# Statistics, query weights and a key projection placed elsewhere in the opening of a pre-norm attention and bilinear GLU kernel

## The chip, the cores and the metric

The kernel runs on one core of one Trainium2 chip. The metric is the device time of one execution in microseconds (us); the numbers compared are medians of several executions. A core has TensorE (PE: matmuls, PEld: its weight loads), VectorE (DVE), ScalarE (ACT), GpSimd (POOL) and SyncE, which here issues all transfers (SPq). Each engine runs its own instructions in the order in which the program hands them out, and waits on semaphores for the others.

## The reference, cut to what matters

```
h  = x + A(layernorm(x)) ;  out = h + B(layernorm(h))        x: 2048 tokens x 576
A(x): q = x @ wq (32 heads of 18), k = x @ wk, v = x @ wv (one key and value head for all)
      softmax(q k^T * 18**-0.5) v, heads joined, @ wo
B(x): ((x @ w_gate) * (x @ w_up)) @ w_down                   width 4608
layernorm(x) = (x - mean) / sqrt(var + 1e-5)
```

Everything is fp32. Most products are done as two or three matmuls in the fast fp32r form, of a high part and a low remainder of each operand.

## The kernel before

The tokens are four blocks of 512, and each block four tiles of 128 (tile 7 is block 1's last, tile 11 block 2's last). `blocks` and `ffn` hold the long part: for each head group and each 128 keys a pair of scores on PE (`pair`: two steps `pr` = 0, 1), an exponential on ACT, and four matmuls with the values (`flush`), among which the GLU's matmuls are spread. Before that comes `keys_values`, the opening, some 60 us, in which every instruction's place is written by hand; all that the change touches lies there. There is no scheduler: the order of the calls is the order on every engine.

What the opening does for each block b of tokens:

- Mean and variance of each tile: `stats` (DVE, bn_stats twice and bn_aggr) or `stats_act` (ACT: a pass that sums, a small one that makes the bias, a pass of squares; the two passes write into a junk tile). `scale` makes 1/sqrt(var + eps) of several tiles in some 17 small instructions on POOL (or DVE). `apply` normalises two tiles on DVE (L204) and two on ACT (L206).
- `turns`: PE transposes the four tiles into PSUM, tiles tr (two, each two banks, tag "s") and trt (tag "m"). `parts`: ACT casts them into high parts (L88, L97), DVE makes the low parts (L89, L98); the result is XT of this block.
- `project(b)`: 14 matmuls psk give keys, values and the last four heads' queries. `keys(b)` makes from it kk (ACT L260), a copy kvq (ACT L262) and, by transfers, the kT that scores read. `values(lo, hi)`: PE transposes values into psv, and DVE copies them into V (L287).
- For block 0 also `query(i)`: 14 matmuls psq, i = 0 to 3, with the weights of seven heads each. These weights are cast by `highs` (the high part) and `lows` (the low part, POOL). `ready(i)` takes psq out of PSUM (cast, then DVE L89) and stores the queries; `bounds` (matmul psg) makes a bound of the scores for the softmax.

[...] Scores and tr share two double banks (tag "s"); trt, psb, psv of blocks after the first and psk of block 3 use one bank (tag "m"); the accumulator of the values has one (tag "a"), which psk of blocks 0 and 1 uses before; psq, the first psg and psk of block 2 share two banks (tag "f"). A tile of a tag takes a bank only when the last reader of the tile that had it is done:

```
    def ps_f(self, name):
        return self.ps.tile([P, TB], F32, tag="f", bufs=2, name=name)
```

`some(gen, n)` issues the next n steps of a generator, `drain` all that are left. `step(work, n)` is a first score, n steps of work, a second score, and the value matmuls of all pending 128 keys but the last. In the profile the scores are s (L608), the exponentials P (L609), the value matmuls acc (L613).

Of the kernel before, what the change touches and what calls it, by code (L numbers as in the profile page):

```python
# [54 lines left out]
class Block:  # L55
# [78 lines left out]
    def keys_values(self, others):  # L134

        pe, act, dve, sp, pool = self.pe, self.act, self.dve, self.sp, self.nc.gpsimd
# [35 lines left out]
        def stats(lo, hi):  # L172
            for j in range(lo, hi):
                b, s = divmod(j, NQ)
                self.ln_stats(xs[b][:, s, :], mv[:, j, :], s, f"a{b}")

        def stats_act(lo, hi):

            junk = self.pp.tile([P, D], F32, tag="P", name="lnjunk")
            x = lambda j: xs[j // NQ][:, j % NQ, :]  # L180
            for j in range(lo, hi):
                act.activation(junk, x(j), AF.Copy, scale=1.0 / D, accum_out=mv[:, j, 0:1])
            for j, less in zip(range(lo, hi), (kab, kabq)):
                act.activation(less, mv[:, j, 0:1], AF.Copy, scale=-1.0 / ROOT_D)
            for j, less in zip(range(lo, hi), (kab, kabq)):
                act.activation(junk, x(j), AF.Square, bias=less, scale=1.0 / ROOT_D, accum_out=mv[:, j, 1:2])

        def scale(lo, hi, eng):
            r = self.rstd(mv[:, lo:hi, 1], f"a{lo}", eng, hi - lo)
            n = self.lp.tile([P, NQ], F32, tag="n", name=f"n{lo}")[:, :hi - lo]  # L190
            if eng is pool:
                pool.tensor_tensor(n, mv[:, lo:hi, 0], r, ALU.mult)
                pool.tensor_scalar(n, n, -1.0, None, ALU.mult)
            else:
                dve.scalar_tensor_tensor(n, mv[:, lo:hi, 0], -1.0, r, ALU.mult, ALU.mult)
            for j in range(lo, hi):
                rs[j] = r[:, j - lo:j - lo + 1], n[:, j - lo:j - lo + 1]

        def apply(b, *of, on=None):
            for s in of:  # L200
                xh = xhs[s] = self.pp.tile([P, D], F32, tag="P", name=f"xh{b}_{s}") if b < 2 else xs[b][:, s, :]
                r, n = rs[NQ * b + s]
                if on is dve:
                    dve.tensor_scalar(xh, xs[b][:, s, :], mv[:, NQ * b + s, 0:1], r, ALU.subtract, ALU.mult)  # L204
                else:
                    act.activation(xh, xs[b][:, s, :], AF.Identity, bias=n, scale=r)  # L206
# [37 lines left out]
        def project(b):  # L244
            psk = psks[b] = (self.ps_a if b < 2 else self.ps_m if b == NB - 1 else self.ps_f)(f"psk{b}")
            for i, (w, m) in enumerate(highs_first(w_h, w_l, self.XT[b])):
                pe.matmul(psk[:6 * DH], w, m, start=(i == 0), stop=(i == 13))  # L247
                yield
# [33 lines left out]
        def values(lo, hi):  # L282
            psv = (self.ps_m if lo else self.ps_a)(f"psv{lo}").rearrange("p (t c) -> p t c", c=64)[:, 0:hi - lo]
            for t in range(lo, hi):
                b, q = divmod(t, NQ)
                pe.transpose(psv[:, t - lo, 0:44], self.kvq[KV, b, q * P:(q + 1) * P], self.ident[KV, KV])
            dve.tensor_copy(self.V[:, lo:hi, 1:1 + DH], psv[:, :, 44 - DH:44])  # L287

        def highs(i, cast):
            cast(self.wq_h[cols[i]], wqr[i])  # L290

        def lows(i):
            pool.tensor_tensor(self.wq_l[cols[i]], wqr[i], f32(self.wq_h[cols[i]]), ALU.subtract)

        def query(i):
            psq = psqs[i] = self.ps_f(f"psq0_{i}")
            for k, (w, m) in enumerate(highs_first(self.wq_h[cols[i]], self.wq_l[cols[i]], self.XT[0])):
                pe.matmul(psq[:7 * DH], w, m, start=(k == 0), stop=(k == 13))
                yield

        def ready(i, copy):
            qs = self.qb.tile([P, 2, TB], F32R, tag="qs", bufs=QS, name=f"qs0_{i}")
            self.split(qs[:7 * DH, 0], qs[:7 * DH, 1], psqs.pop(i)[:7 * DH], copy)
            if i == 0:
                yield
            yield from self.store_q(0, 7 * i, 7, qs, 0 if i else 4)

        def some(gen, n=1):
            for _ in range(n):
                next(gen, None)  # L310

        def step(work=iter(()), n=0):
            self.pair()
            some(work, n)
            self.pair()
            self.flush(len(self.pend) - 1)

        q0, q1, q2, q3 = (query(i) for i in range(4))
# [17 lines left out]
        lows(1)  # L336
        highs(2, act.copy)
        lows(2)
        stats(5, 8)
        scale(4, 8, pool)  # L340
        drain(project(0))
        mean()
# [7 lines left out]
        stats(9, 10)  # L350
        t0 = ready(0, act.copy)
        some(t0, 2)
        some(g0)
        some(t0)
        some(k0)
        some(q1, 6)
        self.bounds(0, act.copy, self.pp.tile([H, 2, TB], F32R, tag="P", name="m2_0"), G0)
        apply(1, 0, 1, on=dve)
        apply(1, 2, 3)
# [6 lines left out]
        some(t0)  # L366
        t1 = ready(1, act.copy)
        some(t1)
        stats(11, 12)
        scale(8, 12, pool)  # L370
        highs(3, pool.tensor_copy)
        lows(3)
        some(q2, 3)
        values(0, 4)
        turns(1)
        parts()
# [15 lines left out]
        some(t2)  # L392
        some(k1)
        some(q3, 4)
        step(q3, 0)
        values(4, 8)
        drain(project(2))
        apply(3, 0, 1, on=dve)
        apply(3, 2, 3)
        drain(t1)  # L400
# [5 lines left out]
        k2 = keys(2)  # L406
        some(k2, 3)
        self.last_heads(0)
        step()
        step(others, 2)  # L410
        drain(project(3))
        k3 = keys(3)
# [851 lines left out]
def f32(ap):  # L1264
    return ap.bitcast(F32)
# [10 lines left out]
def highs_first(W, Wl, XT):  # L1276

    p = passes(W, Wl, XT)
    return p[0:12:3] + p[2:12:3] + p[1:12:3] + p[12:]
# [7 lines left out]
def drain(gen):  # L1287
    for _ in gen:
        pass
# [76 lines left out]
```

## Time and profile before

| | |
|---|---|
| median of 3 runs | 2278.04 us (2277.4 to 2278.1) |
| the profiled execution | 2278.2 us, its span 2276.3 us (1.9 us lie outside the span) |
| PE busy | 2255.7 us, 99% |
| ACT, DVE, POOL busy | 1416.2, 1206.0, 758.9 us |
| granted TensorE clock, mean | 0.999 |

The span runs from the first to the last instruction. Busy times of PE have modelled ends, so "99%" says that PE has few long gaps, not that it streams at its peak. The times in the rows further on count from the start of the span.

### The profile page before, as it was taken

Reading aid. Unit: us, or ns where it says so; the run is one execution under the profiler, and the core shown is the slowest. Engines: PE = TensorE matmul, PEld = TensorE weight load, DVE = VectorE, ACT = ScalarE, POOL = GpSimd, SP = SyncE. Lnnn points to the kernel's source line nnn. Section 1 sums busy time; section 2 is a strip of 40 time slices with the busy share of each in tenths; the row PEclk is TensorE's granted clock in tenths of the full one; section 3 lists DMA queues with packets and bytes.
Section 4 is the critical chain, followed back from the end, with each engine's and each line's share of the span. In section 5 each row is a group of like instructions: output and inputs, shape, how many; then the busy total and the mean of one; then the engine's idle time right before and its main releaser. Section 6 shows DMA issues by size and latency. Waiting matters only on the chain.

```text
span 2276.3 us, 45913 instructions
## 1 busy us (share of the span) xinstructions
PE 2255.7 (99%) x18106; PEld 1602.0 (70%) x18106; DVE 1206.0 (53%) x2131; ACT 1416.2 (62%) x1844; POOL 758.9 (33%) x902
## 2 busy tenths in 40 slices
PE   8999999999999999999999999999999999999998
PEld 5433345777777767677777777777777788888887
DVE  7332435566656577444544455444445476566565
ACT  6899887666676666767666666666676533232332
POOL 4000003565565554232222232223222233333342
PEclk9999999999999999999999999999999999999999
DMA  5222314444333344533333343634333355655553
GB/s 176 84 75 72 112 30 137 152 137 151 136 125 127 137 159 141 205 116 123 115 119 104 121 135 119 194 126 125 104 121 109 122 171 178 209 172 172 181 187 109
DMA packets 127273, 306.75 MB, mean 135 GB/s; under 512 B 17569, under 2 KB 17697, under 8 KB 126409
## 3 DMA queue, kind: packets, MB, share of 16 engines
q1 hardware_dynamic: 127049, 303.73, 40.9%
q8 instruction: 145, 2.38, 0.4%
q14 instruction: 79, 0.65, 0.1%
HBM read 233.76 MB, written 55.67 MB: 127 GB/s over the span
## 4 chain that ended last, share of the span: by engine, by line
PE 95%; DVE 2%; DMA 1%; ACT 1%; issue 0%; SPq 0%; POOL 0%; DVEq 0%; ACTq 0%
PE acc L613 20%; PE pg L1002 20%; PE y L962 17%; PE gu L1002 13%; PE s L608 12%; PE pu L1002 6%; PE yo L766 3%; PE psq L460 2%; DMA X<-X 1%; PE y L920 1%; ACT P L609 1%; DMA x<-in_x_dram 0%; DVE XT L89 0%; PE psk L247 0%; PE ye L920 0%
## 5 line engine op out<-in xcount | busy, mean ns | idle before, releaser
L609 ACT ACTIVATE P<-s 128x1024 f32<-128x1024 f32 x1024 | 1035.7, 1027 | 282.4 <-PE s L608 185.4
L1002 PE MATMUL pg<-X,ws 64*128 64x512 f32 x2592 | 702.6, 389 | 0.1
L1002 PE MATMUL pu<-X,ws 64*128 64x512 f32 x2592 | 702.3, 389 | 0.2 <-DMA X<-X 0.2
L1002 PEld LDWEIGHTS pg<-X,ws 64*128 64x128 f32 x2592 | 479.3, 185 | 69.4 <-issue 1.2
L1002 PEld LDWEIGHTS pu<-X,ws 64*128 64x128 f32 x2592 | 477.2, 185 | 21.2 <-DVE h L767 1.3
L613 PE MATMUL acc<-P,V 128*32 128x512 f32 x4096 | 487.5, 598 | 0.0
L608 PE MATMUL s<-q,kT 56*128 56x512 f32 x2048 | 446.9, 416 | 2.3 <-ACT P L609 1.6
L962 PEld LDWEIGHTS y<-wdo,room 128*128 128x128 f32 x2856 | 386.1, 188 | 46.6 <-issue 45.8
L962 PE MATMUL y<-wdo,room 128*128 128x288 f32 x2856 | 402.7, 300 | 0.0
L969 ACT COPY tmp<-y 128x288 f32<-128x288 f32 x408 | 163.0, 400 | 329.7 <-PE y L962 313.2
L608 PEld LDWEIGHTS s<-q,kT 56*128 56x128 f32 x2048 | 209.4, 184 | 177.9 <-ACT P L609 95.1
L1002 PE MATMUL gu<-X,ws 64*128 64x512 f32 x2592 | 301.7, 389 | 0.6 <-DMA X<-X 0.6
L613 PEld LDWEIGHTS acc<-P,V 128*32 128x32 f32 x4096 | 114.0, 109 | 241.3 <-issue 231.3
L1002 PEld LDWEIGHTS gu<-X,ws 64*128 64x128 f32 x2592 | 246.7, 184 | 49.7 <-issue 4.7
L88 POOL CAST ws<-wr 128x1152 fp32r<-128x1152 f32 x144 | 172.5, 1198 | 319.9 <-PE pu L1002 165.0
L970 POOL TENSOR_TENSOR x<-x,tmp 128x288 f32<-128x288 f32 x204 | 159.2, 809 | 358.9 <-ACT tmp L969 358.1
L970 POOL TENSOR_TENSOR h<-h,tmp 128x288 f32<-128x288 f32 x204 | 159.1, 809 | 305.9 <-ACT tmp L969 305.5
L89 DVE TENSOR_TENSOR ws<-wr,ws 128x1152 fp32r<-128x1152 f32 x144 | 219.6, 1525 | 76.1 <-POOL ws L88 76.1
L1036 DVE TENSOR_TENSOR hf<-pu,g 128x512 f32<-128x512 f32 x96 | 66.3, 691 | 360.1 <-ACT g L1032 359.8
L965 DVE TENSOR_TENSOR x<-x,y 128x288 f32<-128x288 f32 x272 | 117.5, 453 | 146.4 <-PE y L962 146.4
L965 DVE TENSOR_TENSOR h<-h,y 128x288 f32<-128x288 f32 x272 | 118.2, 454 | 111.7 <-PE y L962 108.7
L88 ACT CAST room<-hf 128x256 fp32r<-128x256 f32 (+1 forms) x144 | 73.9, 513 | 55.9 <-DVE hf L1036 55.4
(182 smaller groups left out, 1676.8 us busy)
## 6 DMA issues: line engine op xcount, KB each, us to landing
wdo<-wd_dram SPq DMA_DIRECT2D x369, 288.0 KB
wr<-in_wgu_dram SPq DMA_DIRECT2D x144, 576.0 KB
wd_dram<-wdo SPq DMA_DIRECT2D x123, 288.0 KB
q<-q_dram SPq DMA_DIRECT2D x64, 216.0 KB
raw<-in_wd_dram SPq DMA_DIRECT2D x36, 288.0 KB
q_dram<-qs SPq DMA_DIRECT2D x15, 504.0 KB
X<-X SPq DMA_DIRECT2D x24, 256.0 KB
ob<-ob SPq DMA_DIRECT2D x121, 36.0 KB
```

What stands on the lines that cost most here:

```text
L88: (copy or self.cast)(hi, src)
L89: self.dve.tensor_tensor(lo, src, f32(hi), ALU.subtract)
L608: self.pe.matmul(s_[:, i], self.kT[o:o + 56, t * P:(t + 1) * P], q[o:o + 56, pr], start=True, stop=True)
L609: self.act.activation(p_, s_, AF.Exp, scale=SCALE)
L613: self.pe.matmul(acc[32 * j:32 * j + 32, :], self.V[:, t, :], Ps[j // 2][:, j % 2, :], start=(t == 0), stop=(t == NT - 1), skip_group_chec ...
L766: pe.matmul(y[:, :HD], m, k, start=(i == 0), stop=(i == len(ms) - 1))
L962: pe.matmul(y[:, :HD], m[:, t * P:(t + 1) * P], k, start=(first and j == 0), stop=(j == 2), skip_group_check=True)
L965: dve.tensor_tensor(hs, hs, y[:, :HD], ALU.add)
L969: act.copy(z, y[:, :HD])
L970: pool.tensor_tensor(hs, hs, z, ALU.add)
L1002: pe.matmul(ps, w[o:o + 64, wk, c], X[o:o + 64, xk, c], start=(j == 0), stop=(j == 26))
L1036: dve.tensor_tensor(hf, pu, g, ALU.mult)
```

## The change

Six edits, all in the opening:

1. The last query weights (i = 3) are cast by ACT (`highs(3, act.copy)`) right after those of i = 2, and their low part follows on POOL. Before, POOL did both later, behind `scale(8, 12)`.
2. The statistics of tile 7 go from DVE to ACT.
3. Those of tile 11 go from DVE to ACT, to a place behind the cast of the first query.
4. Eight in place of six matmuls of psq 1 stand ahead of the first `bounds`, and five in place of three of psq 2 ahead of `values(0, 4)`.
5. The key projection of block 2 stands between the two scores of a pair, in place of behind `values(4, 8)`.
6. At a later pair all pending value matmuls come between the two scores, in place of behind them.

```diff
         lows(2)
-        stats(5, 8)
+        highs(3, act.copy)
+        lows(3)
+        stats(5, 7)
+        stats_act(7, 8)
         scale(4, 8, pool)
         drain(project(0))
...
         some(t0, 2)
+        stats_act(11, 12)
         some(g0)
         some(t0)
         some(k0)
-        some(q1, 6)
+        some(q1, 8)
         self.bounds(0, act.copy, self.pp.tile([H, 2, TB], F32R, tag="P", name="m2_0"), G0)
...
         some(t1)
-        stats(11, 12)
         scale(8, 12, pool)
-        highs(3, pool.tensor_copy)
-        lows(3)
-        some(q2, 3)
+        some(q2, 5)
         values(0, 4)
...
         some(q3, 4)
-        step(q3, 0)
+        self.pair()
+        drain(project(2))
+        self.pair()
+        self.flush(len(self.pend) - 1)
         values(4, 8)
-        drain(project(2))
         apply(3, 0, 1, on=dve)
         apply(3, 2, 3)
...
         self.last_heads(0)
-        step()
+        self.pair()
+        self.flush(len(self.pend))
+        self.pair()
         step(others, 2)
```

On PE, around the first `bounds` (psg), the order before, with psb the small matmul for the bound of the keys and tr the transposes of block 1:

```order
L298 MATMUL psq_1_317<-XT_100,wq_h 126x512 x3
L276 MATMUL psb_322<-kab,C 128x1
L298 MATMUL psq_1_317<-XT_100,wq_h 126x512
L298 MATMUL psq_1_317<-XT_100,wq_l 126x512 x4
L298 MATMUL psq_1_317<-XT_100,wq_h 126x512
L491 MATMUL psg_0_346<-tq_0_331,G_136 32x512
L298 MATMUL psq_1_317<-XT_100,wq_h 126x512 x4
L298 MATMUL psq_1_317<-XT_100,wq_l 126x512
L298 MATMUL psq_2_410<-XT_100,wq_h 126x512 x3
L286 MATMUL psv_414<-C,kvq 128x44 x4
L213 MATMUL tr_0_420<-C,xh_0_351 128x128 x4
```

and of the change:

```order
L298 MATMUL psq_1_319<-XT_100,wq_h 126x512 x3
L276 MATMUL psb_324<-kab,C 128x1
L298 MATMUL psq_1_319<-XT_100,wq_h 126x512
L298 MATMUL psq_1_319<-XT_100,wq_l 126x512 x4
L298 MATMUL psq_1_319<-XT_100,wq_h 126x512 x3
L496 MATMUL psg_0_354<-tq_0_333,G_136 32x512
L298 MATMUL psq_1_319<-XT_100,wq_h 126x512 x2
L298 MATMUL psq_1_319<-XT_100,wq_l 126x512
L298 MATMUL psq_2_410<-XT_100,wq_h 126x512 x4
L298 MATMUL psq_2_410<-XT_100,wq_l 126x512
L286 MATMUL psv_416<-C,kvq 128x44 x4
L213 MATMUL tr_0_422<-C,xh_0_359 128x128 x4
```

Two matmuls of psq 1 moved ahead of psg, and two more of psq 2 stand between psg and the transposes.

On PE, from the end of query 3's middle part to block 3's transposes (tr_0_631), the order before; psk_610 is block 2's projection, psv_604 the transposes of the values 4 to 7:

```order
L298 MATMUL psq_3_538<-XT_100,wq_h 126x512 x2
L608 MATMUL s_0_1_0_589<-q_0_368,kT 128x512 x2
L608 MATMUL s_0_1_1_594<-q_0_368,kT 128x512 x2
L613 MATMUL acc_0_599<-P_0_0_0_529,V 32x512 x2
L613 MATMUL acc_0_599<-P_0_0_1_534,V 32x512 x2
L286 MATMUL psv_604<-C,kvq 128x44 x4
L247 MATMUL psk_610<-XT_102,wk 108x512 x14
L213 MATMUL tr_0_631<-C,x_108 128x128 x8
```

and of the change:

```order
L298 MATMUL psq_3_538<-XT_100,wq_h 126x512 x2
L613 MATMUL s_0_1_0_589<-q_0_374,kT 128x512 x2
L247 MATMUL psk_594<-XT_102,wk 108x512 x14
L613 MATMUL s_0_1_1_609<-q_0_374,kT 128x512 x2
L618 MATMUL acc_0_614<-P_0_0_0_529,V 32x512 x2
L618 MATMUL acc_0_614<-P_0_0_1_534,V 32x512 x2
L286 MATMUL psv_619<-C,kvq 128x44 x4
L213 MATMUL tr_0_631<-C,x_108 128x128 x8
```

The fourteen matmuls of the projection moved ahead of the second score, the value matmuls and the transposes psv.

On ACT, the same stretch stands the same in both, here of the change (P_0_1_1 waits for the second score, and x_108 is what `apply` normalises for block 3):

```order
L88 CAST qs_2_578<-psq_2_410 126x512
L614 ACTIVATE P_0_1_0_590<-s_0_1_0_589 128x1024
L614 ACTIVATE P_0_1_1_610<-s_0_1_1_609 128x1024
L206 ACTIVATE x_108<-x_108,n_513,ya_496 128x576 x2
L88 CAST XT_658<-tr_0_631 128x4x256
```

What moved here is only the work that P_0_1_1 waits for. On DVE the order of that stretch is also the same in both: the low parts of block 2 (L89 twice, L98), the low part of query 2 (L89 qs), the copy into V (L287), then block 3's tokens 0 and 1 (L204).

## Rows read from the trace of the kernel before

**Rows 1.** Busy times, from the page: engine, us, share of the span, instructions.

```profile
PE 2255.7 (99%) x18106; PEld 1602.0 (70%) x18106; DVE 1206.0 (53%) x2131; ACT 1416.2 (62%) x1844; POOL 758.9 (33%) x902
```

**Rows 2.** The opening as one stretch: us, busy PE, PEld, DVE, ACT, POOL, granted clock, DMA, GB/s.

```profile
11.18:70.85 59.67, 57.02 (x334) 37.18 (x334) 42.72 (x82) 40.81 (x59) 19.85 (x58) 1.00 0.42 137
```

**Rows 3.** The chain that ended last, at 35 us: start, us, what.

```profile
34.76 0.24 POOL n L193
```

**Rows 4.** Timeline, 13 to 28 us: start, us, engine, line, operation, count, [idle before].

```profile
13.28 4.16 POOL L293 TENSOR_TENSOR wq_l<-wqr,wq_h 128x630 fp32r<-128x630 f32 x3
...
14.66 0.75 ACT L290 CAST wq_h<-wqr 128x630 fp32r<-128x630 f32 x1
...
17.96 0.60 ACT L252 ACTIVATE kvq<-psk 108x512 f32<-108x512 f32 x1 [2.55 <-PE psk L247]
...
18.89 0.77 DVE L103 BATCH_NORM_STATS2 bsa<-x 128x6 f32<-128x288 f32 x2
...
19.93 0.15 DVE L253 TENSOR_SCALAR nmean<-ksum 44x1 f32<-44x1 f32 x1
...
20.99 0.86 PE L298 MATMUL psq<-XT,wq_h 128*126 128x512 f32 x3
...
22.22 0.35 PE L276 MATMUL psb<-kab,C 44*128 44x1 f32 x2 [0.37 <-DVE kab L274]
...
23.76 0.40 PE L298 MATMUL psq<-XT,wq_h 128*126 128x512 f32 x1
...
24.16 0.68 DVE L440 SCALAR_TENSOR_TENSOR tq<-qs 126x512 fp32r<-126x512 f32 x1
...
24.89 0.42 PE L491 MATMUL psg<-tq,G 126*32 126x512 f32 x1 [0.74 <-DVE tq L440]
...
26.69 0.96 PE L298 MATMUL psq<-XT,wq_h 128*126 128x512 f32 x3 [0.23 <-DVE m L89]
...
27.95 1.97 PE L213 MATMUL tr<-C,xh 128*128 128x128 f32 x16
```

**Rows 5.** Timeline, ACT from the statistics of tiles 12, 13 to P.

```profile
31.38 0.71 ACT L182 ACTIVATE lnjunk<-x 128x576 f32<-128x576 f32 x1
...
34.70 0.19 ACT L186 ACTIVATION_READ_ACCUMULATOR lnjunk<-x,kabq 128x1 f32 x1
...
35.02 1.63 ACT L206 ACTIVATE x<-x,n,ya 128x576 f32<-128x576 f32 x2
...
36.68 0.69 ACT L260 ACTIVATE kk<-psk,nmean 44x512 fp32r<-44x512 f32 x1
```

**Rows 6.** Timeline, 38 to 56 us, around block 2's projection and block 3's transposes.

```profile
38.96 2.01 PE L213 MATMUL tr<-C,x 128*128 128x128 f32 x16
...
42.69 0.50 PE L608 MATMUL s<-q,kT 56*128 56x512 f32 x2
...
43.54 0.49 PE L608 MATMUL s<-q,kT 56*128 56x512 f32 x2 [0.35 <-DVE XT L89]
...
43.97 1.06 PE L613 MATMUL acc<-P,V 128*32 128x512 f32 x8
44.24 0.69 DVE L89 TENSOR_TENSOR qs<-psq,qs 126x512 fp32r<-126x512 f32 x1
...
44.96 0.44 PE L286 MATMUL psv<-C,kvq 44*128 44x44 f32 x4
...
45.34 3.49 PE L247 MATMUL psk<-XT,wk 128*108 128x512 f32 x14
45.44 0.23 DVE L287 COPY V<-psv 128x72 f32<-128x72 f32 x1 [0.51 <-PE psv L286]
...
45.59 1.06 DVE L204 TENSOR_SCALAR x<-x,mv,ya 128x576 f32<-128x576 f32 x2
...
48.66 1.91 PE L213 MATMUL tr<-C,x 128*128 128x128 f32 x16
...
55.37 0.18 PEld L460 LDWEIGHTS psr<-XT,wq_h 64*126 64x126 f32 x1 [0.46 <-DVE qs L89]
```

## The prediction

> **What bounds the kernel now.** Read the busy times first [rows 1]: PE has work during 99% of the span, so a microsecond saved or lost anywhere on PE's path should come out at the end unchanged. Then take the opening alone as a stretch [rows 2]: from the first transposes at 11.18 to 70.85 us PE is busy for 57.02 of 59.67 us at a granted clock of 1.00, so visible idle time is only 2.65 us. The six edits lie in this stretch, and the program behind it is the same. That sets the scale: 0.2% of this kernel, about what a measurement of it can tell from no change, is 4.56 us, more than all the idle time that could be removed there. Next, the chain of waits that ended last: at 35 us it runs through POOL's last small instruction of a `scale` [rows 3], so PE is not alone on the path; DVE, POOL and ACT take turns on it. What follows is a walk along those turns with the timeline [rows 4 to 6]. It is made against the profiled execution, 2278.2 us, which lies 0.2 us above the median of 2278.04; I carry the shift over to the median.
>
> **First part: up to block 1's transposes (edits 1, 2, 4).** The cast that goes to ACT takes some 0.75 us, by its neighbour at 14.66, and statistics of one tile some 1.8 us: two took from 31.38 to 34.89 [rows 5]. Behind the cast that ends at 15.41 they would end at about 17.9, and ACT's next instruction, kvq, waits for PE until 17.96 anyway [rows 4]. That wait is the cover; with nothing of it left, up to 2.5 us would go onto kvq and the mean of the keys behind it. I take nothing. The extra low part on POOL, a third of 4.16, ends at about 18.9, when tile 7's statistics must be there too. DVE's tile 7 stood from 18.89 to 19.93 [rows 4]; without it DVE's next ones come 0.94 earlier, and tq ends at 23.90 in place of 24.84.
>
> PE had waited at psb for the bound of keys; now only for its own three matmuls, from 20.99 on, to end, so psb goes from 22.22 to 21.88 (0.34 earlier). Its sixth psq 1 matmul started at 23.76 and now starts at 23.42, the two added ones take 0.235 each (14 of the psk matmuls took 3.49, the last one's tail included [rows 6]), and psg starts at 24.13 in place of 24.89: 0.76 earlier, no longer waiting for tq. Behind psg stands a fixed chain: the ACT cast m, the DVE remainder m, then psq 2, which takes psg's bank and started at 26.69, just when that remainder ended [rows 4]. So psq 2 also comes 0.76 earlier, but now with two more matmuls ahead of the transposes, 0.47. Block 1's transposes start 0.29 earlier (27.66 for 27.95).
>
> **Second part: ACT up to block 2's transposes (edits 1, 3).** From there ACT works without a break; all of it moves by 0.29. One wait goes as well: at 35.02 ACT started to normalise block 2 when POOL's `scale` had just ended (35.00 [rows 3]), while its own statistics had ended at 34.89; instructions of ACT overlap by 0.1, so it could have started at 34.79. POOL waited for tile 11 on DVE, which is now on ACT some 7 us earlier, where ACT has nothing else to do before psg at 24.13. That gives 0.23. Then kk waited for psk, 36.68 against 36.55 at which ACT was free [rows 5]; psk of block 1 is 0.76 earlier now (0.29, and the two psq matmuls that are done already), so another 0.13. P follows, and with it block 2's transposes, which wait for P to free their banks: 0.65 earlier, 38.31 for 38.96 [rows 6].
>
> **Third part: the moved projection (edit 5).** Here the gain is lost. psk of block 2 takes a bank of tag "f". There are two; psq 3, half done, holds one, and psq 2 the other. The last reader of psq 2 is the DVE instruction L89 that makes query 2's remainder, which ran from 44.24 to 44.93 [rows 6], behind all three low parts of block 2. Before, psk came at 45.34, when this was over. Now PE reaches it right after the first score, at 42.04 (42.69 less 0.65), plus some 0.33 (my estimate of a step to operands of another shape; from a score to acc it was 0.43); and must wait for that reader, now ending at 44.28. PE stands still for 1.9 us, where before it did the second score, the value matmuls and psv.
>
> What is queued behind psk on PE: the second score, acc, psv, the transposes of block 3. psk starts at 44.34; its last matmul starts 13 x 0.235 later, at 47.39; the steps between the next ones are those of before: the score again some 0.33 after that, acc 0.43 after the score (43.54 to 43.97), psv 0.99 after acc (to 44.96), DVE's copy V 0.48 after psv (to 45.44) [rows 6]. So V starts at 49.62. And who waits for V: DVE's normalising of block 3's tokens 0 and 1 stands behind it, 0.15 later and 1.06 long. Before, all of that (45.44 to 46.65) lay under the 3.3 us of psk. Now psk has been spent, and nothing covers it: tokens 0 and 1 are ready at 50.34 and 50.83, and the second half of the first transposes starts at 50.89. Before it started at 48.66 + 4 x 0.114 (16 of them took 1.91) = 49.12 [rows 6]. That is 1.77 later. ACT waits for the late second score too, and normalises tokens 2 and 3 by 50.8; just in time.
>
> **Behind it (edit 6).** The rest is a chain of the same length as before, ACT's casts of block 3, DVE's low parts, the remainder of query 3 and psr, which waited for it at 55.37 [rows 6]. The eight value matmuls (0.99) that now stand between two scores fill the wait of the second one, but psr's wait for DVE ends no sooner. Bounds: 0, or a gain of a second wait like that between 42.69 and 43.54, less the 0.23 that a score takes, 0.6. I take 0, since DVE ends last.
>
> **The sum.** First part -0.29, second -0.36, third +2.42: +1.77 on 2278.2 gives 2280.0 for a profiled execution, and 2279.8 for the median. Bounds: with edits 1 to 4 worth nothing, +2.4 (2280.4); with edit 6 worth its 0.6 and the first part 0.3 better, +0.9 (2278.9).
>
> [...] PE stands for 1.9 us and soon after for another 0.8 with little to do. No row of this kernel shows what such a gap does to the clock: the longest wait of PE among these rows is the 0.74 ahead of psg [rows 4], and the granted clock stays 1.00 [rows 2].
> [...]
>
> **Rivals.**
> *The clock falls in the new gap (slower by over 0.2%).* [...] For it: the longest gap so far. Against it: the clock kept 1.00 through every shorter one. Chance 0.04.
> *The projection finds its bank free, so that it does fill a wait of PE.* Then psk starts at 42.37, V at 47.65 and the second half of the transposes at 48.92, 0.2 earlier than before: 2277.8. Even so nothing is won, since tokens 0 and 1 still come behind psk. For it: only that the bank might be free sooner, were DVE's reader ahead. Against: that reader stands last in DVE's order. Chance 0.15.
> *The statistics on ACT push its own path.* If kvq slips, or the cast of psg waits behind tile 11, the first 0.65 is gone and the third part stays: +2.4, or up to +3.2: 2280.4 to 2281.2. For it: a margin of 0.1 us at 17.96. Against: DVE would not take the mean before 19.0 anyhow. Chance 0.13.
> *A gain above 4.56 us.* It would need more than the idle time of the whole opening; 0.01.
>
> **How the numbers follow.** My forecast of +0.9 to +2.4 has 0.67. All cases but the first and last rival lie within 0.2%: 0.95 for same; 0.04 slower, 0.01 faster. For 8 in 10 I reach from the second rival, 2277.7, to the middle of the third, 2280.9.
>
> **What would show it.** Right: psg at about 24.1; block 2's transposes at about 38.3; a wait of PE of about 2 us for DVE L89 just ahead of psk of block 2; V at about 49.6; block 3's transposes waiting for DVE L204; psr at about 57.1, and every later row 1.8 later than before. Wrong: psk of block 2 starting before 44, a granted clock below 1.00 between 44 and 48, or kvq later than 18.2.

## The result: 5.3 us slower, against 1.8 predicted

The changed kernel takes 2283.40 us at the median of 16 runs (2281.88 to 2284.43), the kernel before 2278.06 us (16 runs, 2277.40 to 2279.06): a ratio of 1.0023, with a 95% interval of 1.0015 to 1.0030. The prediction was 2279.8 us, 2277.7 to 2280.9. The profiled execution after has a span of 2281.6 us and took 2283.4. Busy times after, as in [rows 1]:

```profile
PE 2258.8 (99%) x18106; PEld 1608.5 (70%) x18106; DVE 1205.7 (53%) x2125; ACT 1419.5 (62%) x1855; POOL 757.8 (33%) x901
```

TensorE (PE) has the same number of instructions and 3.1 us more busy time; ScalarE (ACT) has 11 more, VectorE (DVE) 6 fewer, GpSimd (POOL) one fewer. Three stretches of the trace show where the time goes. First the start, timeline of PE, before:

```profile
7.36 3.56 PE L321 MATMUL warm<-C 128*128 128x128 f32 x16 [7.36 <-DMA C<-in_cst_dram]
11.18 2.02 PE L213 MATMUL tr<-C,xh 128*128 128x128 f32 x16 [0.25 <-DVE xh L204]
```

and after:

```profile
8.14 3.68 PE L321 MATMUL warm<-C 128*128 128x128 f32 x16 [8.14 <-DMA C<-in_cst_dram]
11.90 2.85 PE L213 MATMUL tr<-C,xh 128*128 128x128 f32 x16
...
15.89 0.48 PE L247 MATMUL psk<-XT,wk 128*108 128x512 f32 x1 [0.27 <-ACT XT L88]
```

The constants landed 0.78 us later, and the same 16 transposes took 2.85 us, not 2.02, so psk of block 0 starts at 15.89, against 14.36 before: 1.53 us of the 5.3 in this one execution. The pace of the transposes changes where the trace has its first record of the full granted clock, at 13.75 us: the 128x128 matmuls start 213 ns apart until then and 109 ns apart after it; in the trace of before that record stands at 10.68, ahead of all 16, and there too they start 109 ns apart after it and the warm-up's 213 ns apart before it. No edit comes ahead of it, and a second profile of the same kernel (below) has 14.55. So from here on I count from psk of block 0 and keep the start apart. Second, the timeline of the first two parts of the prediction, to lay beside [rows 4] and [rows 5]:

```profile
19.18 0.19 ACT L186 ACTIVATION_READ_ACCUMULATOR lnjunk<-x,kab 128x1 f32 x1
19.42 0.60 ACT L252 ACTIVATE kvq<-psk 108x512 f32<-108x512 f32 x1
...
25.51 0.40 PE L496 MATMUL psg<-tq,G 126*32 126x512 f32 x1
...
35.75 0.18 ACT L186 ACTIVATION_READ_ACCUMULATOR lnjunk<-x,kabq 128x1 f32 x1
35.84 1.61 ACT L206 ACTIVATE x<-x,n,ya 128x576 f32<-128x576 f32 x2
37.48 0.69 ACT L260 ACTIVATE kk<-psk,nmean 44x512 fp32r<-44x512 f32 x1
...
39.76 2.01 PE L213 MATMUL tr<-C,x 128*128 128x128 f32 x16 [0.30 <-ACT P L614]
```

psg comes 9.62 us after psk of block 0 (10.53 before), with no wait; kvq comes 3.53 us after it (3.60), so the added statistics fit into kvq's wait; ACT normalises block 2 straight behind its own statistics. Third, the moved projection, to lay beside [rows 6]:

```profile
43.51 0.50 PE L613 MATMUL s<-q,kT 56*128 56x512 f32 x2
...
45.05 0.69 DVE L89 TENSOR_TENSOR qs<-psq,qs 126x512 fp32r<-126x512 f32 x1
...
45.79 3.48 PE L247 MATMUL psk<-XT,wk 128*108 128x512 f32 x14 [1.78 <-DVE qs L89]
...
49.20 0.50 PE L613 MATMUL s<-q,kT 56*128 56x512 f32 x2
...
50.63 0.44 PE L286 MATMUL psv<-C,kvq 44*128 44x44 f32 x4
...
51.11 0.23 DVE L287 COPY V<-psv 128x72 f32<-128x72 f32 x1 [5.38 <-PE psv L286]
51.26 1.06 DVE L204 TENSOR_SCALAR x<-x,mv,ya 128x576 f32<-128x576 f32 x2
...
51.98 1.94 PE L213 MATMUL tr<-C,x 128*128 128x128 f32 x16 [0.90 <-DVE x L204]
...
58.71 0.18 PEld L465 LDWEIGHTS psr<-XT,wq_h 64*126 64x126 f32 x1 [0.62 <-DVE qs L89]
```

psk stands 1.78 us for the reader of query 2's bank, V stands behind it, and the transposes of block 3 wait for the normalising behind V. psr, the last row of the opening, comes 42.83 us after psk of block 0, against 41.01 before: 1.82 us later, where 1.77 was predicted. But from psr to the end of the span it takes 2222.86 us, and 2220.94 before. In this long part, whose program no edit touches, 1.92 us more go. That was not predicted, and the experiments are mostly about it.

### The profile page after: what moved, and what is told of

It is laid out like the page before. It is cut to its first block, busy times and chain, and to the rows that moved or that the text cites. A ratio compares the mean times of both kernels' runs of the same rounds, so it can differ in the third digit from the quotient of the medians.

```text
span 2281.6 us, 45920 instructions
## 1 busy us (share of the span) xinstructions
PE 2258.8 (99%) x18106; PEld 1608.5 (70%) x18106; DVE 1205.7 (53%) x2125; ACT 1419.5 (62%) x1855; POOL 757.8 (33%) x901
## 4 chain that ended last, share of the span: by engine, by line
PE 96%; DVE 1%; ACT 1%; DMA 1%; issue 0%; SPq 0%; DVEq 0%; ACTq 0%
PE pg L1007 20%; PE acc L618 20%; PE y L967 17%; PE gu L1007 13%; PE s L613 12%; PE pu L1007 5%; PE yo L771 3%; PE psq L465 2%; PE y L925 1%; DMA X<-X 1%; ACT P L614 1%; PE psk L247 0%; PE psq L298 0%; PE ye L925 0%; ACT XT L88 0%
## 5 line engine op out<-in xcount | busy, mean ns | idle before, releaser
L89 DVE TENSOR_TENSOR ws<-wr,ws 128x1152 fp32r<-128x1152 f32 x144 | 219.8, 1526 | 75.2 <-POOL ws L88 75.2
```

Of the source, the lines that this page charges most:

```text
L89: self.dve.tensor_tensor(lo, src, f32(hi), ALU.subtract)
```

## The experiments

Times are medians (lowest to highest, number of runs); each kernel was timed beside the one before on the same chip. Three numbers are read from each trace: psk of block 0 (the start), from there to psr (the opening; 41.01 us before), from psr to the end (the long part; 2220.94 us before). They come from one execution each: the nine traces in which the long part is not lost spread from 2220.19 to 2221.43 us, the six in which 1.2 us or more of it are lost from 2222.12 to 2223.13 (the run with seven small instructions stands apart).

### Which edits cost: one part of the change at a time

The changed kernel with the third block's keys left where they were:

```
-        self.pair()
-        drain(project(2))
-        self.pair()
-        self.flush(len(self.pend) - 1)
-        values(4, 8)
+        step(q3, 0)
+        values(4, 8)
+        drain(project(2))
```

> The change without edit 5: block 2's projection is back behind the transposes of the values. Theory A (the walk of the prediction holds in the opening, and what was measured beyond its +1.8 comes from elsewhere and comes again with any edit): the opening gains 0.65 to 0.75, but the time is still 2.5 to 3.5 above the kernel before, 2280.6 to 2281.6. Theory B (all of the +5.3 hangs on the moved projection): 2277.3. Theory C (edits 1 to 4 cost something that the walk left out, such as loads that arrive later): block 0's projection starts 1 us or more later than 14.4, and the time is 1 to 3 above the kernel before.

2279.36 us (2278.82 to 2280.00, 11 runs), ratio 1.0006 (0.9997 to 1.0015). Opening 40.38 (0.63 us gained, as expected), long part 2222.46 (1.52 lost). The gain is lost again in the long part. Two more profiles of this opening, further on, have 40.28; those with the opening of before lie between 40.68 and 41.16.

The kernel before with the projection alone moved (the same lines the other way round):

> The kernel before with edit 5 alone. By the walk of the prediction the second half of block 3's transposes comes 2.4 later than before (1.77 without the 0.65 of edits 1 to 4). Theory A: 2278.06 + 2.4 + about 3.5 of elsewhere = 2284. Theory B: all of the loss is here, 2284 too, but with a start as before and a shift that grows only behind the projection. If the walk is all there is: 2280.5.

2280.87 us (2279.57 to 2282.36, 11 runs), ratio 1.0013 (1.0004 to 1.0022). Opening 44.97 in the profiled execution (3.96 lost), long part 2220.50 (nothing lost). The opening loses more than the walk's 2.4 because something else happened there, as the windows of this profile show: stretch in us, busy PE, PEld, DVE, ACT, POOL (instructions), granted clock, DMA share, GB/s.

```profile
44.00:46.00 2.00, 0.90 (x4) 0.71 (x5) 1.02 (x2) 0.37 (x1) 0.00 (x0) 1.00 0.08 27
46.06:49.48 3.42, 3.42 (x9) 2.38 (x9) 0.00 (x0) 0.00 (x0) 0.00 (x0) 0.50 0.68 236
49.48:53.00 3.52, 2.62 (x18) 1.00 (x17) 0.99 (x3) 2.34 (x3) 0.00 (x0) 1.00 0.00 0
```

Its psk in the timeline:

```profile
45.10 5.07 PE L247 MATMUL psk<-XT,wk 128*108 128x512 f32 x14 [1.80 <-DVE qs L89]
```

After the wait of 1.80 us the granted clock fell to one half (0.50 in the second row) at 46.06, with the projection under way, and came back at 49.48. The 14 matmuls took 5.07 us in place of 3.48: 1.59 us, and 3.96 less 1.59 is the walk's 2.4. In the profile of the changed kernel the same stretch has 1.00 throughout, after a wait of 1.78.

The kernel before with eight of the projection's matmuls done twice, a plain delay of PE at the same place:

```
-            for i, (w, m) in enumerate(highs_first(w_h, w_l, self.XT[b])):
+            ms = highs_first(w_h, w_l, self.XT[b])
+            if b == 2:
+                for w, m in ms[:8]:
+                    pe.matmul(psk[:6 * DH], w, m, start=True, stop=True)
+            for i, (w, m) in enumerate(ms):
```

> The kernel before with eight of block 2's projection matmuls done twice: PE is held for 8 x 0.235 = 1.9 us at the place where the change loses, and no order, engine or bank changes. If a delay of the opening is carried to the end as it is: 2280.0. If a delay there costs more than itself in the long part (the shift of the change grew from 3.35 at 58 us to 5.0 at 1812 us in its trace): 2281.5 to 2282.

2279.39 us (2278.87 to 2280.41, 11 runs), ratio 1.0007 (0.9998 to 1.0016). Opening 42.37 (1.36 lost), long part 2220.19. A delay in the opening is carried to the end and not enlarged, as the prediction assumed.

The changed kernel once more:

> The changed kernel once more, for a second trace. If its late start (block 0's projection at 15.89 in place of 14.36, with the third token tile's load 1.65 later and the clock at its high level at 13.75 in place of 10.68) belongs to the kernel, it comes again; if it is a matter of the single execution, the start is near 14.4 or anywhere between, and the time of that execution is lower by that. The median: 2283.4 again.

2282.79 us (2281.59 to 2283.80, 11 runs), ratio 1.0023 (1.0013 to 1.0032). Start 14.55, opening 42.83 (again 1.82 lost), long part 2222.41 (1.47 lost). So the walk repeats to a hundredth, the late start does not repeat, and the long part's loss does.

### What the long part loses

In these traces the loss grows in steps of up to 0.3 us at the same places, whenever the edits to the statistics and the weights are in. One of them, ACT's timeline at a copy of y, before:

```profile
1250.17 0.40 ACT L969 COPY tmp<-y 128x288 f32<-128x288 f32 x1 [2.93 <-PE y L962]
1251.02 1.22 ACT L969 COPY tmp<-y 128x288 f32<-128x288 f32 x3 [0.44 <-PE y L962]
```

and after, with PE's weight load behind it:

```profile
1254.84 0.40 ACT L974 COPY tmp<-y 128x288 f32<-128x288 f32 x1 [0.44 <-PE y L967]
1255.51 0.70 ACT L974 COPY tmp<-y 128x288 f32<-128x288 f32 x2 [0.28 <-POOL x L975]
1255.97 2.19 PEld L967 LDWEIGHTS y<-wdo,room 128*128 128x128 f32 x16 [0.24 <-ACT tmp L974]
```

Three copies ran back to back; now there is a pause behind the first, and PE waits for the copy after it. The trace names POOL's addition as what ended the pause, but the copy waits for that engine in both kernels alike. Three theories stood: the six buffers of the pool P are turned on by two, since each added statistics call takes one; ACT has eleven more instructions; or the converted weights.

The kernel before with the two buffers taken and not used:

```
         stats(5, 8)
+        for i in range(1):
+            self.pp.tile([P, D], F32, tag="P", name=f"turna{i}")
...
         some(t0, 2)
+        for i in range(1):
+            self.pp.tile([P, D], F32, tag="P", name=f"turnb{i}")
```

> The kernel before, in which two tiles of the pool P are taken and never used, at the two places where the change takes one for the junk output of ScalarE's statistics. No instruction is added; every later tile of P lies two of the six buffers further on, as in the changed kernel. Three theories of why the 1024 steps of the long part lose 1.5 to 1.9 us more when the edits to the statistics and the weights are in. Buffers: it is the turn of P's six buffers, so this kernel loses it as well: the opening's rows as before, the last heads' rows 1.5 us later, 2279.4 us. Count: ScalarE's seven more instructions put what interrupts it in other places of the program; this kernel has none of them, 2277.9 us, no growth. Weights: it comes with the conversion of the last query weights on ScalarE; 2277.9 us too.

2278.12 us (2277.69 to 2278.86, 11 runs), ratio 1.0001 (0.9992 to 1.0010). Opening 41.09, long part 2221.42. Not the buffers.

The first of these kernels with four more taken, so that the turn is as before:

```
         stats_act(11, 12)
+        for i in range(4):
+            self.pp.tile([P, D], F32, tag="P", name=f"turn{i}")
```

> The changed kernel with the third block's keys left where they were (as in the first of these runs), and four more tiles of P taken and never used, so that with the change's two it is six and every later tile of P lies in the buffer that it has in the kernel before. Buffers: the opening's gain of 0.65 us stays to the end, 2277.3 us. Count and weights: 2279.4 us, as without the four.

2279.36 us (2278.28 to 2280.55, 11 runs), ratio 1.0007 (0.9998 to 1.0016). Opening 40.28, long part 2222.64: the loss stays. That excludes the buffers from the other side.

The first edit alone (the conversion of the last query weights on ACT):

```
         lows(2)
+        highs(3, act.copy)
+        lows(3)
...
-        highs(3, pool.tensor_copy)
-        lows(3)
```

> The kernel before with the first edit alone: the last query weights converted by ScalarE straight after the third ones, their low part straight after, and nothing more on GpSimd. ScalarE has one instruction more, GpSimd one less, no buffer of P is taken. Opening: a few tenths either way. Weights: the long part grows by 1.5 us, 2279.4 us. Buffers: no growth, about 2277.8 us. Count: one instruction moves less than seven, between 2277.8 and 2279.4 us.

2277.74 us (2277.00 to 2278.56, 11 runs), ratio 0.9999 (0.9990 to 1.0008). Opening 41.05, long part 2220.86. Not the weights. ACT's trace has as many records here as before (3070): one conversion more, one record of a semaphore less.

The kernel before with seven small ACT instructions (seven was my count of what the change adds; its trace has eleven more):

```
+        tiny = p0.tile([P, 8], F32, name="tiny")
...
         stats(5, 8)
+        for i in range(4):
+            act.copy(tiny[:, i:i + 1], mv[:, 0, 0:1])
...
         some(t0, 2)
+        for i in range(4, 7):
+            act.copy(tiny[:, i:i + 1], mv[:, 0, 0:1])
```

> The kernel before with seven more ScalarE instructions, copies of one column, four of them where the change puts its first statistics and three where it puts the second; no buffer of P is taken. They delay the opening by at most about the ScalarE time that they take, which I look at apart: what counts is how much the shift grows between the end of the opening and the last heads. Count: it grows by 1.5 us or so, some 2279.5 us. Buffers and weights: it does not grow, 2278 us.

2287.24 us (2286.80 to 2287.70, 5 runs), ratio 1.0040 (1.0026 to 1.0054). Opening 41.03, long part 2230.29: 9.35 us lost, six times what was expected. Two things are mixed here. The groups of matmuls with the largest busy time (busy us, mean ns of one), in this kernel

```profile
L1007 PE MATMUL pg<-X,ws 64*128 64x512 f32 x2592 | 709.3, 392 | 0.1
L1007 PE MATMUL pu<-X,ws 64*128 64x512 f32 x2592 | 708.3, 392 | 0.3
```

and before

```profile
L1002 PE MATMUL pg<-X,ws 64*128 64x512 f32 x2592 | 702.6, 389 | 0.1
L1002 PE MATMUL pu<-X,ws 64*128 64x512 f32 x2592 | 702.3, 389 | 0.2 <-DMA X<-X 0.2
```

show matmuls of the gate and up projections 3 ns longer, 12.7 us of busy time, all through the long part. Why is not shown. The runs with 57 and 63 copies and no new tile keep 389, so my guess is the new tile of 32 bytes for each partition; no run tests it by itself. So this run doesn't count for the theories by its time. But it led to the pattern: laid beside the trace of before, ACT's extra idle times stand 128 records apart.

### ScalarE's idle times, 128 records apart

Number ACT's records in a trace from 0, and look at those whose number is 63 more than a multiple of 128. Between the record before and such a record ACT is often idle for 0.25 to 0.36 us, mostly 0.32, far more often than ahead of others. From 100 us on:

```
kernel                    ACT records  such pauses  of them ahead of P or tmp  mean of the other 127 places
before                    3070         8 of 23      4                          1.7
projection alone          3070         8 of 23      4                          1.7
weights alone             3070         8 of 23      4                          1.7
changed                   3081         14 of 23     14                         1.6
projection back           3081         15 of 23     14                         1.7
```

At the other places ACT is idle for longer (over 0.36 us: 7 in the kernel before, 4 in the changed one) or goes on with less than 0.15 us of idle time (8 and 5); for the short ones no row gives the reason. In the kernel before, only 4 of the pauses stand ahead of P or tmp. Eleven more records move each to another instruction, and in the changed kernel 14 stand ahead of the exponentials (P) and the copies of y (tmp), for which PE waits. The row at 1255.51 above is record 1855 = 14 x 128 + 63.

The traces also show what the pauses cost. Lay the starts of PE's matmuls behind psr against those of the same matmuls before: in the changed kernel the shift grows by 0.2 to 0.3 us at nine of the 14 pauses, 2.3 to 2.6 us in all, and shrinks by 0.3 to 0.6 us in all at the places where the kernel before has its own pauses. That makes about 2 us, against the 1.92 and 1.47 lost in the two profiles.

And they show what else happens at these places. The page lists the transfers by queue, one of them named q14 instruction, here of the changed kernel (packets, MB, share of the 16 engines):

```profile
q14 instruction: 79, 0.65, 0.1%
```

These packets have 8192 bytes. At 20 of the 23 places in the changed kernel one of them starts within 2.5 us of the start of the record before, against 2.1 of 23 on average for the other 127 numbers; in the kernel before it is 18 of 23, against 1.9. So packets of this queue come at these places. What makes ScalarE stand there is not shown, since no run changed the packets.

To test that the place of the pauses costs the time, the kernel before gets copies of one column on ACT while it stands idle for its first weights, into elements that are overwritten later:

```
         G0 = self.qb.tile([P, 64], F32R, tag="G0", bufs=1, name="G0")
+        for i in range(11):
+            act.copy(self.kvq[:, NB - 1, i:i + 1], self.V[:, 0, 0:1])
```

> The kernel before with eleven copies of one column on ScalarE, written into elements that are overwritten later, while it stands idle from 2.0 us on for the first weights: no address, no order and no buffer changes, and every later ScalarE instruction has a number higher by eleven, as in the changed kernel. Pause: in the traces so far ScalarE pauses by about 0.32 us at each record whose number is 63 more than a multiple of 128; in the kernel before most of these fall on waits, in the changed one among the copies of y and the exponentials that TensorE waits for. By this the eleven copies cost what the changed kernel loses in the long part: opening's rows as before, growth by about 1.5 us until the last heads, some 2279.4 us. Chance or the statistics' buffers: 2277.9 us.

2280.32 us (2279.83 to 2280.73, 11 runs), ratio 1.0010 (1.0001 to 1.0019). Opening 40.68, long part 2223.13 (2.19 lost). The shortest of these runs is longer than the longest of the kernel before beside them (2279.10). 15 of 23 places show the pause, and the copies of y have it where the changed kernel has it:

```profile
1251.76 0.70 ACT L971 COPY tmp<-y 128x288 f32<-128x288 f32 x2 [0.28 <-POOL x L972]
```

With `range(57)`:

> The same with 57 copies, some 0.09 us each, so still done by about 7.3 us and nothing later for them. Pause: adding up the pauses that would fall where the kernel before has no wait of ScalarE to take them up gives 2.3 us as it is, 4.3 us with eleven more instructions, 3.1 us with 57; scaled by the 1.5 us that eleven cost, growth by about 0.6 us, 2278.5 us. If it were the copies' number or work that costs, five times the eleven's: more than 2280 us. Buffers: 2277.9 us.

2278.10 us (2277.65 to 2278.73, 11 runs), ratio 1.0000 (0.9991 to 1.0009). Opening 41.16, long part 2220.40. 9 of 22 places show the pause, 8 of them ahead of P or tmp, so the count alone does not give the cost; PE's matmuls, below, do. The copies of y from above are back to back again:

```profile
2.02 5.42 ACT L171 COPY kvq<-V 128x1 f32<-128x1 f32 x57
...
1250.46 1.23 ACT L971 COPY tmp<-y 128x288 f32<-128x288 f32 x3 [0.44 <-PE y L964]
```

Five times as many copies cost nothing where eleven cost 2.2 us; even the 0.6 us that I had expected did not show. By the matmuls' starts the pauses cost PE 0.5 us here, and 0.6 come back at the places of before.

With `range(63)`:

> The same with 63 copies, done by about 7.8 us. Pause: the same sum is 5.0 us with 63, near the largest of all the 128 places that it can have; growth by 1.4 to 2.0 us, some 2279.6 us, though it is only six copies more than the run with 57. If number or work costs: as that run and a tenth more. Buffers: 2277.9 us.

2279.97 us (2279.28 to 2280.45, 11 runs), ratio 1.0008 (0.9999 to 1.0017). Opening 41.08, long part 2222.12 (1.18 lost). 16 of 22 places. Six copies more than the run before, 1.9 us at the median, and no run of the one is as short as the longest of the other. It is the place and not the number. (21 of the 22 places have a packet of that queue behind them here, 19 of 22 with 57 copies: the packets move with the records.)

The changed kernel with the projection left where it was and 46 copies, which with its own eleven make 57:

> The changed kernel with the third block's keys left where they were, and 46 such copies at the start, which with its own eleven make 57. Pause: it keeps the opening's gain of 0.65 us and grows by about 0.6 us and not by 1.5, so about 2278 us. Buffers or statistics: as without the copies, 2279.4 us.

2277.43 us (2276.58 to 2278.44, 11 runs), ratio 0.9998 (0.9989 to 1.0007). Opening 40.28, long part 2220.71. The opening's gain of 0.7 us now reaches the end; without the 46 copies it was 2279.36, and the runs of the two don't overlap (on two chips, where the kernel before has 2278.15 and 2277.88). By its median this is the lowest of all, though the interval doesn't tell it from the kernel before.

### What is left for the moved projection

The whole change with the 46 copies:

> The whole change with 46 copies of one column on ScalarE at its idle start, so that its pauses fall as in the run with 57. Pause: the 2.2 us that eleven copies cost come back, 2283.2 less 2.0 to 2.2 makes 2281.1 us; what is left over the kernel before is the moved projection's 3 us. If the whole change loses by something else than the pauses: 2283 us.

2280.70 us (2279.70 to 2282.11, 11 runs), ratio 1.0011 (1.0002 to 1.0020). Opening 43.03 (2.02 lost), long part 2221.36 (0.42 lost). That is 2.7 and 2.1 us less than the two sets of the change as it was, more than the long part's 1.5 to 1.9. All 11 runs have a mean granted clock of 0.999, which allows a fall of the clock or none, so a part of the difference may be the clock's.

The same with six matmuls that nobody reads in the gap. If a fall of the clock, as in the profile of the projection moved alone, plays a part in the times, the runs come out shorter and closer together:

```
         self.pair()
+        fill = self.ps_m("fill")
+        for i in range(6):
+            pe.matmul(fill[:6 * DH], w_h[:, 0], self.XT[2][:, 0], start=True, stop=True)
         drain(project(2))
```

> The same, and six more matmuls of 128x512 (1.5 us) into a bank of their own, whose result nobody reads, just ahead of the moved projection, where TensorE waits 1.8 us for VectorE's read of query 2's bank. [...] If the clock plays no part in the times: 2281.1 us, as without; and if the filling itself delays the projection, up to 0.3 us more.

2280.49 us (2280.16 to 2281.45, 11 runs), ratio 1.0011 (1.0002 to 1.0020). Opening 43.71, long part 2220.80. The filling didn't start at once:

```profile
43.42 1.64 PE L401 MATMUL fill<-XT,wk 128*108 128x512 f32 x6 [1.06 <-DVE XT L98]
44.90 3.41 PE L249 MATMUL psk<-XT,wk 128*108 128x512 f32 x14
```

It waited 1.06 us for the low part of the block's tail, then ran past the end of the old wait: psk starts 30.86 us after psk of block 0, 0.76 later than without. The profile has no fall of the clock, but neither has the one without the filling. The median is 0.2 us lower and the runs are closer together; that is too little to tell.

## Why the prediction was wrong

- **The walk through the opening was right.** The sum was +1.77; both profiles of the changed kernel have +1.82. Its terms hold too: psg without a wait (0.91 us earlier, counted from psk of block 0; 0.76 predicted), kvq not later than its wait for PE, ACT's normalising of block 2 straight after its statistics, psk waiting for DVE's L89 for 1.78 us (1.9 predicted), the transposes of block 3 waiting for L204. The first two parts alone gave 0.63 to 0.73 in three profiles (0.65 predicted).
- **The step that failed is the first paragraph's "the program behind it is the same".** I took it that the long part carries the shift unchanged, and of the prediction's signs the last one, every later row 1.8 later, did not come. A delay is carried so (the run with the matmuls done twice). But ScalarE's eleven more instructions shift every later one against pauses of about 0.32 us whose places lie 128 records apart (14 of 23 show one in the changed kernel, all 14 ahead of P or tmp), and with that 1.5 to 1.9 us go in the long part of the changed kernel. Shown by the copies: eleven lose 2.2 us, 57 nothing, 63 again 1.8, at the medians; and by PE's matmuls, whose shift grows by 0.2 to 0.3 us at nine of the 14 pauses. What makes ScalarE pause is not shown; a packet of 8192 bytes from the queue q14 instruction starts within 2.5 us at 20 of its 23 places.
- **The rival of the clock was real, and too small a chance was given to it.** It got 0.04, on the ground that the clock had kept through every shorter gap. The fall occurred in one profile of the projection moved alone, 0.50 from 46.06 to 49.48 after a wait of 1.80 us, and cost 1.59 us, since part of the projection was done before it began; no run shows a fall that costs the 2.8 us which, beside the walk's 1.77, would make 0.2% (4.56 us). The fall did not occur in two profiles of the changed kernel with the same wait (1.78), so the gap alone doesn't decide it; what does is not shown.
- **In which of the changed kernel's runs it falls.** Of its 27 runs, the 10 whose mean granted clock is 1.000 have medians of 2282.3 and 2282.4 in the two sets, the 12 with 0.998 have 2283.8 and 2283.5. My estimate from these means, rounded as they are: 1.000 leaves less than 2.3 us at half the clock in the whole span, and the fall in the trace above lasted 3.42; 0.998 takes at least 6.8 us, and the stretch at half the clock that ends each of the 16 traces lasts at most 4.23 inside its span (2.59 before, 1.38 after). So by it the 12 had a fall somewhere and the 10 had none like it. Where it came no row shows, for those 12 runs have no trace, and the run with the gap filled did not settle it.
- **The account.** In the second profile of the changed kernel, 1.82 for the opening, 1.47 for the long part and 0.19 for its start make the 3.48 us by which its span exceeds that of before (2279.79 against 2276.31). It was the shortest run of its set. By the medians, the runs without the fall are 4.3 and 4.5 us above the kernel before: 1.82 for the opening, 1.5 to 1.9 for the long part, and 0.5 to 1.2 that stay open. The runs with it are 1.2 and 1.5 us longer, which fits the 1.59 of the fall in the trace above. The rivals of a free bank and of ACT's own path did not occur.

## What to carry to other kernels

In this kernel, adding instructions on an engine that feeds the critical one cost some 2 us in a long unrolled part that the edit never touched, or nothing, by their number: compare that part's length in both traces, apart from the edited stretch, and count the engine's records. Before a small loss is put down to an edit's idea, run the kernel before with as many idle instructions as the edit adds; if the loss comes with them, try other numbers of harmless ones in an idle stretch: here 46 took back 1.9 us with the projection left in place and 2.1 to 2.7 us with it moved. Work that is moved to fill a wait on the critical engine should be followed to its bank's last reader, and to what lay covered under it in the old place.

## What the runs showed of the hardware

- In all 16 traces ScalarE's idle times of about 0.32 us gather ahead of records 191, 319, ... of its own stream (63 more than a multiple of 128): at 8 to 16 of 22 or 23 places from 100 us on, against 1.4 to 1.8 for another number. At one of them, record 1855 of the changed kernel, the trace names POOL as what ended the 0.28 us, though the copies wait for POOL in the kernel before too, where they run back to back. VectorE and GpSimd show no such pattern at that number in three traces (0 or 1 of 20 and of 11 places in those of before and after).
- The start of an execution varies by up to 2.1 us whatever the kernel: among the sixteen traces psk of block 0 starts between 13.77 and 15.89 us. The first record of the full clock stands between 9.55 and 13.75 us in them, and sixteen transposes took 2.02 us where it came ahead of them and 2.85 where it came at 13.75, in their midst.
- Matmuls of 64x512 took 392 ns in place of 389 all through a kernel in which one tile of 32 bytes per partition had been added.
